# Linear-attention state summed over four token tiles per burst instead of two, with two more buffers per ring in a weight slot

## The chip, the cores and the metric

The kernel runs on one core of a Trainium2 chip. The metric is the device time of one execution in microseconds (us). The profile's span is about 1.8 us shorter than the time of the same run.

## The reference, cut to what matters

```python
# A: linear attention, B: dilated sliding-window attention, both on the same x (2048 x 1024, 32 heads of 32)
pq, pk = phi(q), phi(k)                       # phi(t) = where(t > 0, t + 1, exp(t)) + 1e-6
kv = einsum("bhsd,bhse->bhde", pk, v)         # the state: a 32 x 32 sum over all 2048 tokens, per head
z  = einsum("bhsd->bhd", pk)
a  = (pq @ kv) / (pq @ z + 1e-6) @ A_wo
b  = windowed_attention(x) @ B_wo
g  = sigmoid((x * gate_w).sum(-1, keepdims=True))
return g * a + (1 - g) * b
```

## The kernel before

The program is recorded as a list of operations with reads and writes. A list scheduler in Python then fixes the order of each engine before anything is built: an operation's place follows from its dependencies, a planned cost and a priority. The state stage walks over 16 tiles of 128 tokens. For each it computes the features of the keys (`pk`, two groups of eight matmuls) and the values with a column of ones (`az`, two groups). The sum over tokens needs both. A "burst" is the operation that does it: 32 small matmuls per tile, in four column tiles of the tensor engine, whose records overlap in the trace (64 matmuls of 182 ns each start within 0.48 us). In the code, a bank is one of the buffers that matmuls write to, evacuation is the copy of a result out of its bank, `r` counts the four groups of a tile, and `KVAT` is 1.

```python
    pk = Ring([SB([128, 1024], BF16, "pk%d" % i) for i in range(4)])
    az = Ring([SB([128, H, 33], BF16, "az%d" % i) for i in range(4)])
# ... cut ...
        def state(two):                        # the tiles of one burst
            bank = main.next()
            def fn(e):
                for s in range(8):
                    for i, (t, pkt, azt) in enumerate(two):
                        for c in range(4):
                            h = 16 * (s // 4) + 4 * c + s % 4
                            last = e.matmul(bank.ap()[32 * c:32 * c + 32, s * 33:s * 33 + 33], pkt[:, h * 32:(h + 1) * 32], azt[:, h, :],
                                            start=(i == 0), stop=(i == len(two) - 1), tile_position=(0, 32 * c))
                return last
            # ... cut: add() gathers the bank into kva on VectorE ...

        def run_state():
            fn, rd, bank, add = state([states.pop(0)[1] for _ in range(2)])
            P.op("pe", fn, 0.55, mode="k", reads=rd, writes=[bank.iv], name="kv")
            add()

        for t in range(NT):
            # ... cut: the four groups of the tile, their evacuation, attention blocks of B in between ...
                if r == KVAT and t % 2 and t > 1:
                    run_state()

        def last_state():
            run_state()
            totals()
        after(1, last_state)                   # the last burst, one group into the next stage
        load_w(3, 0, Bo, 0, 50)                # B's output weight, 2 MB, as soon as slot 3 is free
        load_w(3, 1, Bo, 512, 51)
```

The attention of B runs in between, in "attention bursts": scores of one block and values of the block before, 32 + 64 small matmuls in 64 x 64 tiles. The folding of the state into A's output weight comes later, in four bursts of 16.

## Time and profile before

| | kernel before |
|---|---|
| time, 3 runs ahead of the prediction | 484.12 us (484.1 to 484.35) |
| span in the profile | 482.1 us |
| tensor engine busy, share of the last chain | 98%, 95% |
| state bursts | 8 of 64 matmuls, 0.70 us each |
| DVE, ACT busy | 58%, 31% |

In the profile, PE is the matmul row of the tensor engine, PEld its weight loads, DVE and ACT are VectorE and ScalarE, SPq is the queue that issues transfers. L1343 is a full-array matmul, L1450 and L1485 are attention's scores and values, L1579 is the state (L1574 after the change). The lines that carry the reading are shown in the prediction.

### The profile page before, as it was taken

To read this page: it belongs to the slowest core of one execution; us is meant where nothing else is said; L and a number is where in the kernel's file an instruction comes from. 1 tells how busy PE (TensorE), PEld (TensorE's weight loads), DVE (VectorE), ACT (ScalarE), POOL (GpSimd) and SP (SyncE) were. 2 spreads that over 40 slices of the span, in tenths; PEclk is the share of its full clock that TensorE was granted. 3 is DMA by queue.
4 is the path that set the end of the run, shared out by engine and by line. 5 is a ranking of instruction groups with operands and counts; after the bars stand their busy time and mean duration, and the time that the engine had idled before them with its cause. 6 is when DMAs were issued, how large, how long until landed. Compare 5 with 4: busy or idle time off the path is not lost.

```text
span 482.1 us, 10165 instructions
## 1 busy us (share of the span) xinstructions
PE 472.3 (98%) x4349; PEld 224.3 (47%) x4403; DVE 280.3 (58%) x578; ACT 149.3 (31%) x238; POOL 5.8 (1%) x36
## 2 busy tenths in 40 slices
PE   8999999999999999999999999999999999999997
PEld 3444444444444544545444555444444444444443
DVE  2121435878687788565747565697489136653434
ACT  2111111235333345435434335345532130111000
POOL 4000000000000000000000000000000000000000
DMA  8999992232014359742213414720186019840212
GB/s 225 218 215 311 357 363 46 65 111 87 1 33 141 87 139 203 163 82 69 76 43 83 101 33 99 215 46 1 15 223 156 0 17 235 228 24 2 88 68 90
DMA packets 72951, 57.39 MB, mean 119 GB/s; under 512 B 37953, under 2 KB 60865, under 8 KB 72898
## 3 DMA queue, kind: packets, MB, share of 16 engines
q1 hardware_dynamic: 72210, 56.07, 45.0%
q8 instruction: 36, 0.59, 0.5%
q10 hardware_dynamic: 688, 0.59, 0.4%
q14 instruction: 17, 0.14, 0.1%
HBM read 34.49 MB, written 13.76 MB: 100 GB/s over the span
## 4 chain that ended last, share of the span: by engine, by line
PE 95%; DVE 2%; ACT 1%; issue 1%
PE ps_all L1343 77%; PE ps_all L1729 11%; PE ps_all L1485 2%; PE ps_all L1450 2%; ACT E L1464 1%; PE ps_all L1382 1%; DVE E L1467 1%; DVE pk L1356 1%; PE ps_all L1579 0%; PE ps_all L1674 0%; DVE qd L1440 0%; PE ps_all L1646 0%; DVE e L1354 0%; DVE rs L1501 0%; DVE ot L1502 0%
## 5 line engine op out<-in xcount | busy, mean ns | idle before, releaser
L1343 PE MATMUL ps_all<-w,xT 128*128 128x512 bf16 x930 | 206.9, 380 | 3.7 <-issue 2.5
L1343 PE MATMUL ps_all<-xT,w 128*128 128x512 bf16 x750 | 165.8, 379 | 1.8 <-issue 1.3
L1343 PEld LDWEIGHTS ps_all<-w,xT 128*128 128x128 bf16 x960 | 92.3, 98 | 110.1 <-issue 1.6
L1343 PEld LDWEIGHTS ps_all<-xT,w 128*128 128x128 bf16 x768 | 74.2, 98 | 89.4 <-issue 1.3
L1729 PE MATMUL ps_all<-w,qT 128*128 128x512 bf16 (+1 forms) x260 | 55.4, 372 | 0.2
L1729 PEld LDWEIGHTS ps_all<-w,qT 128*128 128x128 bf16 x264 | 25.9, 98 | 29.6
L1374 DVE CAST vst<-ps_all 128x512 bf16<-128x512 f32 x15 | 10.4, 694 | 43.1 <-PE ps_all L1343 43.1
L1464 ACT ACTIVATE E<-ps_all 128x1824 bf16<-128x1824 f32 (+1 forms) x18 | 30.4, 1687 | 14.1 <-PE ps_all L1485 14.1
L1354 DVE TENSOR_SCALAR e<-e 128x512 bf16<-128x512 bf16 x64 | 18.5, 289 | 27.4 <-ACT e L1352 13.7
L1733 DVE SCALAR_TENSOR_TENSOR o<-ps_all,gm,xT 128x512 bf16<-128x512 f32 (+1 forms) x25 | 18.0, 728 | 21.1 <-PE ps_all L1729 21.0
L1352 ACT ACTIVATE e<-ps_all 128x512 bf16<-128x512 f32 x32 | 19.1, 597 | 34.8 <-PE ps_all L1343 34.8
L1350 ACT ACTIVATE e<-ps_all 128x512 bf16<-128x512 f32 x32 | 19.1, 597 | 27.6 <-PE ps_all L1343 26.5
L1302 DVE TENSOR_TENSOR mx<-mx,kT 128x1024 bf16<-128x1024 bf16 x32 | 21.0, 684 | 9.8 <-ACT kT L1375 9.6
L1502 DVE TENSOR_TENSOR ot<-ps_all,rs 128x480 bf16<-128x480 f32 (+1 forms) x54 | 25.8, 505 | 0.0
L1375 ACT ACTIVATE az<-ps_all 128x512 bf16<-128x512 f32 x24 | 14.4, 599 | 36.2 <-PE ps_all L1343 36.2
L1501 DVE RECIPROCAL rs<-ps_all 128x15 f32<-128x15 f32 (+1 forms) x54 | 9.4, 203 | 27.8 <-PE ps_all L1485 25.9
L1302 DVE TENSOR_TENSOR mx<-mx,qT 128x1024 bf16<-128x1024 bf16 x32 | 21.0, 684 | 6.8 <-ACT qT L1378 6.7
L1375 ACT ACTIVATE vst<-ps_all 128x512 bf16<-128x512 f32 x17 | 10.2, 599 | 47.5 <-PE ps_all L1343 47.5
L1375 ACT ACTIVATE kT<-ps_all 128x512 bf16<-128x512 f32 x21 | 12.5, 596 | 36.0 <-PE ps_all L1343 36.0
L1378 ACT ACTIVATE qT<-ps_all 128x512 bf16<-128x512 f32 x20 | 11.9, 597 | 34.4 <-PE ps_all L1343 34.4
L1356 DVE SCALAR_TENSOR_TENSOR pk<-ps_all,e 128x512 bf16<-128x512 f32 x32 | 21.6, 678 | 0.2
L1378 ACT ACTIVATE xT<-ps_all,g 128x512 bf16<-128x512 f32 x10 | 6.9, 687 | 45.1 <-PE ps_all L1343 45.1
(73 smaller groups left out, 276.8 us busy)
## 6 DMA issues: line engine op xcount, KB each, us to landing
rb<-rc_hbm SPq DMA_DIRECT2D x32, 256.0 KB, 5.9
w<-in_A_wqkv_dram SPq DMA_DIRECT2D x6, 1024.0 KB, 8.8
v<-vB_hbm SPq DMA_DIRECT2D x36, 132.0 KB, 2.9
vB_hbm<-vst SPq DMA_DIRECT2D x32, 132.0 KB, 5.8
w<-in_B_wqkv_dram SPq DMA_DIRECT2D x4, 1024.0 KB, 8.3
xn<-in_A_x_dram SPq DMA_DIRECT2D x16, 256.0 KB, 2.6
out_dram<-o SPq DMA_DIRECT2D x15, 256.0 KB, 2.2
oB_hbm<-ot SPq DMA_DIRECT2D x36, 96.0 KB, 2.2
```

The costliest lines, as they stand in the source:

```text
L1302: P.op("dve", lambda e, m=m, op=op: e.tensor_tensor(m[:, 0:n], m[:, 0:n], src, op), 0.08 + n / 1920.0, reads=[m.all(), reg], writes=[m.all()],
L1343: last = e.matmul(bank.ap(), lhs(dc), rhs(dc), start=(dc == 0), stop=(dc == 7))
L1350: P.op("act", lambda e: e.activation(e_[:, :], bank.ap(), ACT.Exp), act(512), reads=[bank.iv], writes=[e_.all()])
L1352: P.op("act", lambda e: e.activation(e_[:, :], bank.ap(), ACT.Exp, accum_out=qe[:, col:col + 1]), act(512) + 0.1, reads=[bank.iv], writes= ...
L1354: P.op("dve", lambda e: e.tensor_scalar(e_[:, :], e_[:, :], 1.0, 1e-6, op0=ALU.min, op1=ALU.add), 0.25, reads=[e_.all()], writes=[e_.all()])
L1356: P.op("dve", lambda e: e.scalar_tensor_tensor(out=dst, in0=bank.ap(), scalar=0.0, in1=e_[:, :], op0=ALU.max, op1=ALU.add), dps(512), read ...
L1375: fa = lambda e: e.activation(dst, src(), ACT.Copy)
L1378: fa = lambda e: e.activation(dst, src(), ACT.Copy, scale=scale)
L1464: P.op("act", lambda e: e.activation(E[:, 0:32 * nq].rearrange("p (j q) -> p j q", j=4), ps[:, 4:8, 0:8 * nq], ACT.Exp), act(32 * nq), rea ...
L1502: P.op("dve", lambda e, r=r, src=src, dst=dst, m=m: e.tensor_tensor(dst, src()[:, :, 0:32], r[:, 0:m, None].to_broadcast([128, m, 32]), AL ...
L1729: last = e.matmul(bank.ap(0, f1 - f0), qT[:, dc, t * 128:(t + 1) * 128], ws[3][:, dc, f0:f1], start=(dc == 0), stop=(dc == 7))
L1733: P.op("dve", lambda e, bank=bank, o_=o_, t=t, n=n, i0=i0, i1=i1, tgt=tgt, c0=c0: e.scalar_tensor_tensor(out=o_[:, i0 * 128:i1 * 128].rear ...
```

## The change

Its intent: the tensor engine is the bound, and each burst makes it change its tiling mode twice; half as many bursts pay half as many changes (0.225 us for the two in the trace of before, which is what a burst costs beyond the time from its first start to its last). Four tiles per burst were taken to need six buffers instead of four, and the only free place is the slot of B's key weights, which is later filled with A's output weight. So that load moves behind the last burst that uses the two new buffers.

```diff
-    pk = Ring([SB([128, 1024], BF16, "pk%d" % i) for i in range(4)])
-    az = Ring([SB([128, H, 33], BF16, "az%d" % i) for i in range(4)])
+    pk = Ring([... 4 as before ...] + [SB([128, 1024], BF16, "pk%d" % i, at=ws[1].lo + 2048 * (i - 4)) for i in (4, 5)])
+    az = Ring([... 4 as before ...] + [SB([128, H, 33], BF16, "az%d" % i, at=ws[1].lo + 4096 + 2112 * (i - 4)) for i in (4, 5)])
@@ at the end of the projections
-        for c in range(4): for I in range(2):   # A's output weight into ws[1], 8 transfers of 256 KB
-                P.op("sp", ... A_wo ..., prio=40, chan="wo%d_%d" % (c, I), lat=0.9)
@@
         def run_state():
-            fn, rd, bank, add = state([states.pop(0)[1] for _ in range(2)])
-            P.op("pe", fn, 0.55, mode="k", reads=rd, writes=[bank.iv], name="kv")
+            fn, rd, bank, add = state([states.pop(0)[1] for _ in range(4)])
+            P.op("pe", fn, 1.03, mode="k", reads=rd, writes=[bank.iv], name="kv")
             add()
+        def load_wo():                          # the same 8 transfers
@@
-                if r == KVAT and t % 2 and t > 1:
+                if r == KVAT and t % 4 == 0 and t:
                     run_state()
+                    if t == 12:
+                        load_wo()
```

(The first two lines are shortened, and the transfers' access patterns are left out.)

More of the change, by code (lines that the diff above doesn't have):

```diff
@@ L1215, in build_kernel @@
     mx = [SB([128, 1024], BF16, "mx%d" % i, at=ph + 2048 * i) for i in range(2)]
-    pk = Ring([SB([128, 1024], BF16, "pk%d" % i) for i in range(4)])
-    az = Ring([SB([128, H, 33], BF16, "az%d" % i) for i in range(4)])
+    pk = Ring([SB([128, 1024], BF16, "pk%d" % i) for i in range(4)] + [SB([128, 1024], BF16, "pk%d" % i, at=ws[1].lo + 2048 * (i - 4)) for i in (4, 5)])
+    az = Ring([SB([128, H, 33], BF16, "az%d" % i) for i in range(4)] + [SB([128, H, 33], BF16, "az%d" % i, at=ws[1].lo + 4096 + 2112 * (i - 4)) for i in (4, 5)])
     warm = SB([128, 512], BF16, "warm", at=pk.t[2].lo)
@@ L1558, in plan @@
         top_end(1, ALU.min)
-        for c in range(4):
-            for I in range(2):
-                P.op("sp", lambda e, c=c, I=I: e.dma_start(ws[1][32 * c:32 * c + 32, 4 * I:4 * I + 4, :],
-                                                           A_wo[512 * I + 128 * c:512 * I + 128 * c + 128, :].rearrange("(r e) f -> e r f", e=32)), 0.6,
-                     writes=[ws[1].part((4 * I, 4 * I + 4), (0, 1024))], prio=40, chan="wo%d_%d" % (c, I), lat=0.9)
         load_w(2, 0, Aw, 0, 42)
@@ L1591, in run_state @@
         def run_state():
-            fn, rd, bank, add = state([states.pop(0)[1] for _ in range(2)])
-            P.op("pe", fn, 0.55, mode="k", reads=rd, writes=[bank.iv], name="kv")
+            fn, rd, bank, add = state([states.pop(0)[1] for _ in range(4)])
+            P.op("pe", fn, 1.03, mode="k", reads=rd, writes=[bank.iv], name="kv")
             add()
+        def load_wo():
+            for c in range(4):
+                for I in range(2):
+                    P.op("sp", lambda e, c=c, I=I: e.dma_start(ws[1][32 * c:32 * c + 32, 4 * I:4 * I + 4, :],
+                                                               A_wo[512 * I + 128 * c:512 * I + 128 * c + 128, :].rearrange("(r e) f -> e r f", e=32)), 0.6,
+                         writes=[ws[1].part((4 * I, 4 * I + 4), (0, 1024))], prio=40, chan="wo%d_%d" % (c, I), lat=0.9)
         for t in range(NT):
```

## The prediction

> **What bounds the kernel now.** I read the page's first and fourth parts, then the chain in order of time, then the groups by form, then the timeline of the tensor engine around single state bursts, and last the DMA queue of the weight that moves.
>
> ```profile
> PE 472.3 (98%) x4349; PEld 224.3 (47%) x4403; DVE 280.3 (58%) x578; ACT 149.3 (31%) x238; POOL 5.8 (1%) x36
> ...
> PE 95%; DVE 2%; ACT 1%; issue 1%
> ```
>
> The tensor engine is 98% busy and carries 95% of the chain that ended last. DVE and ACT have room. A busy matmul row can hide slack, so the rate has to be checked. The chain in order of time:
>
> ```profile
> 14.82 10.74 PE ps_all L1343 x49
> 25.61 10.74 PE ps_all L1343 x49
> ```
>
> Two pieces of 50 matmuls each start 10.79 us apart: 0.2158 us per 512-column matmul. Wherever I checked from 129 us on, the start-to-start spacing of the full-array matmuls is this number, with extra time only around bursts of small tiled matmuls (scores and values of attention, the linear-attention state, the fold, the denominators). So the span is nearly a sum: full matmuls at 0.2158 us plus a fixed cost for each burst. A change pays by what it takes out of that sum; work taken from DVE, ACT or DMA pays only if a stall is there, and there is almost none.
>
> The state work, in the groups by form:
>
> ```profile
> L1579 PE MATMUL ps_all<-az,pk 128*32 128x33 bf16 x512 | 5.3, 182 | 0.0
> L1579 PEld LDWEIGHTS ps_all<-az,pk 128*32 128x32 bf16 x512 | 4.5, 93 | 3.4 <-DVE e L1354 2.5 <-issue 0.4 <-DVE ot L1502 0.4
> L1588 DVE TENSOR_TENSOR kva<-ps_all,kva 128x264 f32<-128x264 f32 x7 | 3.0, 423 | 0.6 <-PE ps_all L1579 0.6
> ```
>
> 512 matmuls in 8 bursts of 64; seven adds (and one copy) gather them. The 3.4 us of weight-load idle is 8 times 0.42 and is named after DVE, but I don't read it as a wait for data: the array still streams the last full matmuls in that time. What a burst costs is read from the matmul timeline:
>
> ```profile
> 300.57 3.40 PE L1343 MATMUL ps_all<-w,xT 128*128 128x512 bf16 x15 [0.16 <-issue]
> 303.90 0.67 PE L1579 MATMUL ps_all<-az,pk 128*32 128x33 bf16 x64
> 304.73 0.59 PE L1343 MATMUL ps_all<-w,xT 128*128 128x512 bf16 x2 [0.16 <-issue]
> ```
>
> and the weight loads of the same stretch:
>
> ```profile
> 300.34 3.14 PEld L1343 LDWEIGHTS ps_all<-w,xT 128*128 128x128 bf16 x16
> 303.90 0.57 PEld L1579 LDWEIGHTS ps_all<-az,pk 128*32 128x32 bf16 x64 [0.42 <-DVE e L1354]
> ```
>
> Sixteen weight loads but fifteen matmuls: the first matmul after each burst has no record. Counting the visible gaps on both sides would therefore charge a whole matmul (0.216 us) to the burst. Between the two first records (300.57 and 304.73, both second matmuls of their run) lie 4.16 us with 16 full matmuls, 16 x 0.2158 = 3.45. The burst costs 0.70 us. The same subtraction gives 0.701 to 0.705 for all eight, so none of them waits for anything that another leaves out.
>
> [...] of the 0.70 us, 0.48 lies between the first and the 64th start of the burst, and 0.225 is left for going in and coming back. [...] in every burst the first 32 matmuls [...] start within 0.218 us, 6.8 ns each, and from there on the step is a steady 8.46 ns[...]. [...] The trace shows 36 packets and 0.59 MB on an instruction queue, so 16 KB each; a burst of 128 pairs is just such a block.
>
> **The change part by part.**
>
> 1. Bursts. Before: 8 bursts of 64 matmuls. After: 4 of 128; the number of matmuls is the same, 512. All lies on the tensor engine, which is the bound. One new burst is 0.218[...] + 95 steps x 8.46 ns = 1.022 us, plus 0.225 for the two mode changes: 1.247 us. Two old ones are 1.406. Saved: 0.16 us for each pair, 4 x 0.16 = 0.64 us. It is this small because merging saves a pair of mode changes (0.225) but gives 0.06 of it back[...].
>
> 2. Adds on DVE. Four of the eight go: 4 x 0.42 = 1.7 us. DVE is at 60% in this stage and no matmul waits for it; worth 0.
>
> 3. Two more buffers in each ring, in the slot of the B key weights. The four-tile burst needs them, as it holds four tiles while the next is written. The first burst comes about two groups (3.5 us) after the last of its data is computed; evacuating that takes 0.60 us on ACT or 0.69 on DVE, so no wait. Fourth-tile data before were older still, which saved nothing.
>
> 4. The A output weight (2 MB, 8 transfers) moves from the end of the projection stage to after the third burst.
>
> ```profile
> 174.00:194.00 20.00, 19.68 (x274) 9.82 (x275) 15.98 (x41) 10.04 (x12) 0.00 (x0) 1.00 1.00 195
> 277.00:289.00 12.00, 11.68 (x207) 6.03 (x208) 7.82 (x19) 4.68 (x6) 0.00 (x0) 1.00 0.10 28
> 289.00:301.00 12.00, 11.68 (x236) 6.27 (x237) 6.03 (x18) 5.76 (x8) 0.00 (x0) 1.00 0.42 103
> 301.00:313.00 12.00, 11.58 (x236) 5.95 (x238) 7.81 (x20) 4.30 (x8) 0.00 (x0) 1.00 0.72 217
> ```
>
> The last two columns are DMA share and GB/s. Today it is fetched between 174 and 194 us, where the DMA engines are full at 195 GB/s, and the tensor engine is not held up even there: the attention bursts of that stretch cost 1.15 to 1.26 us against the usual 1.145. In the new place, from some 280 us, the engines are at a tenth. My estimate from 195 GB/s is about 11 us of transfer, landing near 292; the first fold reads it at 319.8. Slack 27 us. Worth 0 at the new place, and at most the 0.1 us of one slow attention burst at the old.
>
> 5. The last burst is 0.54 us longer (64 x 8.46 ns) and the fold depends on it. Today its add starts at 312.98 and the transposed state is ready by 314.8, 5 us before the fold; half a microsecond doesn't reach it.
>
> Sum: 484.12 - 0.64 = 483.48, which I round to 483.5.
>
> **The rivals.**
>
> A. The visible gaps were right and a merge saves more. With 0.309 and 0.344 us read at the burst's two ends, one would get 0.92 per burst and 1.5 us in all: 482.6. Against it speak the sixteen loads to fifteen matmuls. A variant: 7.6 ns average per matmul for the second half too gives 0.225 x 4 = 0.9 us, 483.2.
>
> B. The merged burst waits, for the fourth tile's values or for a bank. A wait of one evacuation, 0.6 to 0.7 us, in each of three bursts would cost up to 2 us: 485.5. For it: the fourth tile is fresh where the tiles of before were old. Against it: two groups of slack, and ACT and DVE have no attention exponentials to do in the fourth tile of each four, since none is issued there.
>
> C. The moved weight delays the value loads of the last attention blocks or comes late for the fold; a stall of 1 to 5 us, 485 to 488. Against it: values are loaded about 16 us ahead, twice the burst of weight traffic, and the tensor engine stood 20 us of full DMA traffic before.
>
> D. Instruction fetch. Three attention bursts of the old kernel (195.7, 226.6, 299.7) hold one gap of 50 to 93 ns and a few smaller ones. A burst of 256 instructions is 1.3 times theirs (192) and may meet one or two more: +0.1 to 0.3 us.
>
> E. The order of instructions is found by a list scheduler at build time, so removing four operations can shuffle others: a group swapped around a burst, another neighbour for a burst. One mode-change pair more or less is 0.2 us; I allow 0.5 either way.
>
> **Range and chances.** The sum gives 483.5. A lowers the lower end to 482.6, D and E with a little of B raise the upper end to 484.3; eight in ten should lie there. Two per cent is 9.7 us. All eight bursts together cost 8 x 0.70 = 5.6 us, so faster by 2% is out of reach of the change itself: 1%. Slower by 2% needs C in a form that nothing shows: 1%. Within 2%: 98%.
>
> **What the new profile should show.** Four state bursts of 128 matmuls, one each some 31 us apart, each with a cost by the same subtraction near 1.25 us (right), above 1.4 (no gain), or near 1.1 (the average rate holds). Full-array spacing stays 0.2158 us. Steps after the 32nd matmul stay at 8.46 ns up to the 128th. The gathering adds fall to three and one copy, with no matmul gaining by it. The A output weight is issued near 280 us and no fold waits for it. I am wrong if the matmul row shows a stall ahead of a state burst named after ACT or DVE of more than 0.2 us, if the attention bursts after 280 us cost more than 1.3 us, or if the time moves by more than 1 us while the bursts' costs come out as said; then the order of something else has changed.

Cut in it, at the marks, are the author's reasons for the cost of a mode change and for the two rates of starts, which no trace or run shows, and a size of the instruction blocks that was not taken from the traces. The trace of before shows 0.218 us to the 33rd start, 8.46 ns a start beyond and 0.225 us left for going in and coming back, so a burst of 128 comes to 1.247 us and the sum to 484.12 - 0.64 = 483.48. The 0.06 us given back are the second 64 matmuls taken at 8.46 ns throughout, where the first 32 of a burst of their own start at 6.8. That a burst of 128 pairs is about a block of instructions is an estimate from the traces: between two of the first 34 fetches lie 127.1 loads on average before the change and 126.8 after, so 254 matmuls and loads; with some two semaphore instructions (64 and 67 records beside the 4403 loads) that is about 256, the figure used below.

## The result, and the profile after

| | before | after |
|---|---|---|
| median of 6 runs each | 484.18 us (483.92 to 484.57) | 484.37 us (483.97 to 484.78) |
| span in the profile | 482.1 us | 483.0 us |

A ratio here is the one of the two kernels' fast runs in the same rounds; it is not quite the ratio of the medians. It is 1.0003, with a 95% interval of 0.999 to 1.0016: the same. 483.5 was predicted with a range up to 484.3; the median lies 0.07 us above the range, and the 0.64 us that should have been saved are not in the time.

The page after the change, engines and chain:

```profile
PE 478.1 (99%) x4403; PEld 223.7 (46%) x4403; DVE 279.6 (58%) x575; ACT 148.7 (31%) x237; POOL 6.2 (1%) x38
...
PE 96%; SPq 2%; DMA 1%; issue 0%; DVE 0%
```

The matmul row grew by 5.8 us because all 4403 matmuls have a record this time, where 54 were missing before (a second trace of the changed kernel, with 50 missing, has 471.6 us). The bound is the same engine. The new entries of SPq and DMA are at the start of the kernel. The groups of the state by form:

```profile
L1574 PE MATMUL ps_all<-az,pk 128*32 128x33 bf16 x512 | 4.9, 184 | 0.2 <-issue 0.2
L1574 PEld LDWEIGHTS ps_all<-az,pk 128*32 128x32 bf16 x512 | 4.4, 93 | 2.0 <-issue 2.0
L1583 DVE TENSOR_TENSOR kva<-ps_all,kva 128x264 f32<-128x264 f32 x3 | 1.3, 433 | 1.0 <-PE ps_all L1574 1.0
```

Three adds instead of seven. The load row's idle time should be 4 x 0.42 = 1.7 us and is 2.0, and the matmul row, which had none, has 0.2 us "issue": time in which the engine waited for nothing that the profile shows. The second burst in the timeline of matmuls:

```profile
245.71 1.03 PE L1343 MATMUL ps_all<-w,xT 128*128 128x512 bf16 x4
246.67 1.20 PE L1574 MATMUL ps_all<-az,pk 128*32 128x33 bf16 x128
247.80 1.47 PE L1343 MATMUL ps_all<-w,xT 128*128 128x512 bf16 x6
```

128 matmuls in one record, and full matmuls again 1.13 us after its start. With 0.09 us of entry (the last full matmul ahead started 0.309 us before the burst, and takes 0.216) that is 1.22. By the subtraction that the prediction uses, which ends at the second full matmul after the burst, it is 1.235, close to the predicted 1.247; all costs below are of this kind. The last burst, in the same view:

```profile
310.18 1.89 PE L1343 MATMUL ps_all<-xT,w 128*128 128x512 bf16 x8
312.00 1.06 PE L1574 MATMUL ps_all<-az,pk 128*32 128x33 bf16 x111
313.25 0.30 PE L1574 MATMUL ps_all<-az,pk 128*32 128x33 bf16 x17 [0.20 <-issue]
313.48 7.08 PE L1343 MATMUL ps_all<-xT,w 128*128 128x512 bf16 x32
```

It is cut in two. After 111 matmuls the engine stands for 0.38 us, start to start, then does the other 17. Its whole cost is 1.48 + 0.09 = 1.57 us (1.587 by the subtraction). No semaphore shows there: in the program all waits of a burst stand ahead of its first matmul, and in the trace, too, the first of the 128 is the only one that carries a wait.

Where the 0.9 us of the longer span came from, read from the starts of single records, in three parts. The start, up to the first attention burst, took 130.17 us instead of 129.09. The middle, from there to the last matmul, took 349.59 instead of 350.02. The end, from there on, took 3.29 instead of 3.02. The order of the built programs is the same for the tensor engine and the transfer queue until long after the start-up loads (in the traces, up to weight load 1699 of the tensor engine and to 174 us on the transfer queue), so the change has no hand in the first part; in the twelve traces that part runs from 129.09 to 130.17, and the trace of the kernel before happens to have the shortest. It has the shortest end, too: 3.02 to 3.33 in the twelve, without a pattern that follows the change. The change is to be judged by the middle: 0.43 us saved of the 0.64.

### The profile page after: what moved, and what is told of

It reads as the page before. It is cut to its first block, busy times and chain, and to the rows that moved or that the text cites. A ratio compares the mean times of both kernels' runs of the same rounds, so it can differ in the third digit from the quotient of the medians.

```text
span 483.0 us, 10222 instructions
## 1 busy us (share of the span) xinstructions
PE 478.1 (99%) x4403; PEld 223.7 (46%) x4403; DVE 279.6 (58%) x575; ACT 148.7 (31%) x237; POOL 6.2 (1%) x38
## 4 chain that ended last, share of the span: by engine, by line
PE 96%; SPq 2%; DMA 1%; issue 0%; DVE 0%
PE ps_all L1343 79%; PE ps_all L1733 11%; PE ps_all L1450 2%; PE ps_all L1485 2%; SPq L1317 1%; DMA w<-in_B_wqkv_dram 1%; PE ps_all L1574 1%; SPq L1322 1%; PE ps_all L1678 0%; PE ps_all L1650 0%; DVE o L1737 0%
## 5 line engine op out<-in xcount | busy, mean ns | idle before, releaser
L1343 PE MATMUL ps_all<-w,xT 128*128 128x512 bf16 x960 | 212.2, 380 | 0.5 <-DMA xT<-in_A_x_dram 0.4
L1343 PE MATMUL ps_all<-xT,w 128*128 128x512 bf16 x768 | 168.3, 380 | 0.0
```

The lines of the kernel that those rows point to most:

```text
L1343: last = e.matmul(bank.ap(), lhs(dc), rhs(dc), start=(dc == 0), stop=(dc == 7))
```

## The experiments

The theory: the sum of burst costs holds, and what is missing from the gain is the gap inside the last burst; the start is chance. The rivals: the changed kernel itself starts slower; the moved weight holds something up; a long burst in that place has the gap for a reason of its own. The "middle" below is always the time from the first attention burst to the last matmul. The state column is the sum over all state bursts by the subtraction. There is one trace of each kernel where the table doesn't say more. How far the middle can be trusted shows in the three traces whose tensor-engine order is that of the kernel before: 349.84 to 350.02. The times are given with the number of runs.

| kernel | state bursts, us | gap in a state burst | middle, us | median, us | before, same rounds |
|---|---|---|---|---|---|
| before | 5.62 | none | 350.02 | 484.18 (6) | |
| changed, three traces | 5.29, 6.33, 5.29 | 0.38, 1.42, 0.39 us | 349.59, 350.78, 349.58 | 484.37 (6), 484.81 (6), 484.24 (5) | 484.18, 484.50, 484.11 |
| last burst split | 5.90 | 0.81 us | 350.17 | 485.10 (5) | 484.50 |
| pairs, buffers and load moved | 5.61 | none | 349.96 | 484.51 (5) | 484.50 |
| fours, four buffers | 5.69 | 0.14, 0.66 us | 350.52 | 484.69 (6) | 484.50 |
| changed, B's weight late, two traces | 4.94, 4.94 | none | 349.20, 349.24 | 483.73 (5), 483.77 (5) | 484.08, 484.11 |
| before, B's weight late | 5.61 | none | 349.84 | 484.31 (5) | 484.08 |
| changed, instructions shifted | 4.99 | none | 349.27 | 483.84 (1) | 484.08 |
| single tiles | 7.40 | 0.32 us | 351.48 | 486.12 (1) | 484.08 |

### The changed kernel again

No edit.

> The changed kernel once more, unaltered. Theory 1 (the sum of burst costs holds; what is missing from the predicted gain is one gap of 0.35 us inside the last state burst, and a start-up stall of some 0.8 us that comes by chance in some executions of either kernel): three state bursts cost 1.235 us each, the last 1.58 with the gap at the same matmul, the times fall into two groups some 0.7 us apart for both kernels, and group against group the changed kernel is 0.2 to 0.4 us faster. Theory 2 (the start-up stall belongs to the changed kernel): only the changed kernel has the upper group, and the kernel before stays within 0.3 us. Theory 3 (the moved weight load holds something up): attention bursts after 275 us cost more than the usual 1.145 us.

Measured: ratio 1.0001 (0.9988 to 1.0015). The three full bursts cost 1.234 to 1.236 us, the last 2.62: the gap stands at the same matmul and is 1.42 us long this time. The matmul timeline of that burst:

```profile
311.70 1.06 PE L1574 MATMUL ps_all<-az,pk 128*32 128x33 bf16 x111
313.99 0.29 PE L1574 MATMUL ps_all<-az,pk 128*32 128x33 bf16 x17 [1.23 <-issue]
```

The kernel before spread nearly as widely in these rounds (483.64 to 485.03 in 11 runs, against 483.73 to 485.35 in 6), so the wide spread does not belong to the changed kernel, and that rival falls; the two clean groups of times that I had expected did not appear either. Attention bursts after 275 us cost up to 1.26 us here but no more than 1.15 in the first trace; the moved weight is no steady cost.

What the place of the gap means shows when the tensor engine's weight loads are counted from the start of the program: the gap follows load 3530 in each of the three traces. Each matmul has one load, and the page's instruction queue shows 36 packets of 16 KB, by the mean distance of two fetches (126.8 loads) about 256 instructions or 128 pairs each. That suggests a fetch that comes late; the next runs test it.

### The last burst split

```diff
+                if r == KVAT and t == 15:
+                    run_state(2)
 ...
         def last_state():
-            run_state()
+            run_state(2)
```

> The last four-tile burst is split into two of two tiles, placed as before; the other three stay merged. Theory 1: state bursts cost 3 x 1.235 + 2 x 0.703 = 5.11 us in all (changed kernel 5.29, kernel before 5.62), no gap inside a burst, so 0.5 us less than the kernel before and 0.2 us less than the changed kernel, outside the start-up. If the gap of the last burst came from where it stands and not from its length, one of the two small bursts still has it and costs about 1.05 us.

The first expectation failed, and the second branch held. The matmul timeline of the last burst, now of two tiles:

```profile
310.57 0.59 PE L1574 MATMUL ps_all<-az,pk 128*32 128x33 bf16 x55
311.79 0.24 PE L1574 MATMUL ps_all<-az,pk 128*32 128x33 bf16 x9 [0.63 <-issue]
```

It has a gap of 0.81 us after its 55th matmul, and load 3530 of the program is just this 55th. So the gap follows neither the burst's length nor the place in the burst: it stays at one place of the instruction stream. The small burst costs 1.50 instead of 0.70 us, and the kernel is slower than the one before (ratio 1.0022, 1.0008 to 1.0036).

### Pairs, with the buffers and the load moved

```diff
-            fn, rd, bank, add = state([states.pop(0)[1] for _ in range(4)])
+            fn, rd, bank, add = state([states.pop(0)[1] for _ in range(2)])
-                if r == KVAT and t % 4 == 0 and t:
+                if r == KVAT and t % 2 and t > 1:
-                    if t == 12:
+                    if t == 13:
```

> Two-tile bursts as in the kernel before, but with the six buffers and the output weight loaded late. Its tensor-engine order is that of the kernel before, instruction for instruction. Theory 1: eight bursts at 0.70 us, the time is that of the kernel before within 0.2 us. Theory 3: slower than the kernel before by 0.3 us or more, with attention bursts above 1.2 us or a wait for the output weight after 275 us.

Eight bursts at 0.70 us, middle 349.96, ratio 0.9999 (0.9986 to 1.0013). Buffers and late load of A's weight cost nothing and give nothing that these runs can show. That rival falls.

### Fours with four buffers

A's output weight is loaded at the old place, the rings have four buffers, and a burst stands ahead of the next tile's first write:

```diff
-                if r == KVAT and t % 4 == 0 and t:
+                if r == 3 and t % 4 == 3 and t < NT - 1:
```

> Four-tile bursts with the four buffers of the kernel before and the output weight loaded where it was. If the extra buffers are needed, each burst has to wait for the values of its fourth tile and the next tile's features wait for the burst: a stall of 0.5 to 2 us at three places, time 1 to 4 us above the kernel before. If the slack of PSUM covers it, bursts cost 1.24 us with no wait and the time is that of the changed kernel within 0.3 us.

The second branch held in the main: no wait of the tensor engine on ACT or DVE at a burst, two middle bursts at 1.234 us, and ratio 1.0006 (0.9992 to 1.0019). So the two extra buffers and the moved load were not needed for bursts of four. Its first burst has a gap of 0.14 us that I did not follow up, and the last has 0.66 us, ending 1.27 us after a block's fetch, between load 3531 and its matmul (one instruction later than in the others; a stream with one instruction less ahead of it would make it the same place, which I did not show). One attention burst (188 us) has a gap of 0.34 us too.

### The changed kernel with B's output weight late

The theory could be made sharper. From the transfer records of the instruction queue, the last fetch ahead of the gap, taken to be that of the block in which the stream goes on after load 3530, began at 310.77, 311.71 and 309.44 us in the first three traces with a gap, and the gap ended 1.51, 1.34 and 1.31 us after the end of that fetch. That is in the 303 to 312 us in which the 2 MB of B's output weight fill the engines (the data queue takes 97.7% of the 16 engines' time in the first trace). Hence the test: take the traffic away.

```diff
         def last_state():
-            run_state()
+            last_kv = run_state()
+            load_w(3, 0, Bo, 0, 50, after=[last_kv])
+            load_w(3, 1, Bo, 512, 51, after=[last_kv])
             totals()
 ...
-        load_w(3, 0, Bo, 0, 50)
-        load_w(3, 1, Bo, 512, 51)
```

> The changed kernel with one thing held back: the B output weight (2 MB) is loaded after the last state burst instead of from 303 us on, when the engines' queues are full while a block of tensor instructions is being fetched. Theory 1, now sharper (the tensor engine runs out of instructions at one fixed place, load number 3530 of its stream, because the fetch of that block waits behind the weight): [...]the last burst costs 1.24 us, all four 4.95 us, no gap inside it, and from the first attention burst to the last matmul it is 0.35 us or more shorter than the changed kernel (349.6 us) and 0.6 to 0.8 us shorter than the kernel before (350.0 us). Rival (the gap belongs to a long burst in this place, whatever the DMA does): the gap stays at the same matmul.

The clause cut in it had the fetch come earlier than 310.8 us, at a place that followed from a view of what starts a fetch, which was not shown.

The last burst in the matmul timeline:

```profile
311.42 1.20 PE L1574 MATMUL ps_all<-az,pk 128*32 128x33 bf16 x128
312.77 1.46 PE L1343 MATMUL ps_all<-xT,w 128*128 128x512 bf16 x6 [0.16 <-issue]
```

The gap is gone: the burst costs 1.235 us by the subtraction (the first full matmul after it has no record), and all four cost 4.94. The DMA queues from 305 to 309.5 us, first in the changed kernel, where no instruction fetch begins in that stretch (queue and kind: packets, MB, share of the engines):

```profile
q1 hardware_dynamic: 1331, 1.35, 98.8%
```

and from 309.5 to 312.5 us, still in the changed kernel, where it does:

```profile
q1 hardware_dynamic: 1022, 0.93, 90.6%
q8 instruction: 1, 0.02, 2.0%
```

With B's weight late, 305 to 309.5 us:

```profile
q1 hardware_dynamic: 1265, 0.45, 59.5%
q8 instruction: 1, 0.02, 1.3%
```

The data queue has gone from 98.8% to 59.5%, and the block comes in that stretch, at 306.97 us instead of 310.77: 3.8 us earlier, and its transfer ends 4.4 us ahead of its use. The place in the stream tells the same. With the weight held back the fetch begins as load 3400 does (0.17 us after it), some 130 loads, about one block, ahead of load 3531; in the changed kernel it begins 3.40 us after load 3400. A trace shows when a fetch begins, not when it was asked for; that it was asked for near load 3400 in both is an inference from the same stream of instructions. How the DMA engines divide their time between the two queues no trace shows; the runs show the later fetch beside the fuller data queue.

The middle is 349.20 us, 0.39 below the changed kernel's first and 0.82 below that of the kernel before. Of the 0.82 the state bursts make 0.68; the rest is as large as the spread of the middle. The ratio to the kernel before is 0.9991 (0.9977 to 1.0004).

### The same hold-back in the kernel before

> The same hold-back in the kernel before, as a control. Theory 1: it had no gap in its state bursts, so nothing changes there: eight bursts at 0.70 us, first attention burst to last matmul 350.0 us within 0.2. If the late weight helps in some other way, it is shorter here too.

No gap, eight bursts at 0.70 us, middle 349.84, ratio 0.9999 (0.9985 to 1.0012): no gain from the late weight where no gap was. Yet the fetch moves here as well, from 309.97 to 306.89 us. So the block was late in the kernel before too. There load 3530 is the 47th of a burst of 64, and load 3531 was needed 1.60 us after the fetch's end: just outside the 1.26 to 1.51 us at which gaps end. The kernel before escapes by 0.1 to 0.3 us.

### The instruction stream shifted

75 more warm-up matmuls at the very start, narrow ones, so that the start takes about as long:

```diff
         for i in range(WARM):
-            P.op("pe", lambda e: e.matmul(banks[7].ap(), warm[:, 0:128], warm[:, :], start=True, stop=True), 0.43, ...)
+            def warm_fn(e, i=i):
+                if i < 2:
+                    return e.matmul(banks[7].ap(), warm[:, 0:128], warm[:, :], start=True, stop=True)
+                for _ in range(10 if i < 5 else 9):
+                    last = e.matmul(banks[7].ap(0, 48)[0:32, :], warm[:, 0:32], warm[:, 0:48], start=True, stop=True)
+                return last
+            P.op("pe", warm_fn, 0.43, ...)
```

> The changed kernel with 75 more (narrow) warm-up matmuls at the start, so 150 more tensor instructions ahead of everything; the weight is loaded where the changed kernel loads it. The ends of the 256-instruction blocks move 150 instructions earlier against the work: the end that stood at the 112th matmul of the last burst now stands at its 37th. Theory 1: [...]no gap in the last burst (1.24 us), or a gap that stands at the 37th matmul; in no case at the 112th. Rival (place and length): the gap stays at the 112th matmul. The whole time is not to be compared, as the start is changed.

The clause cut in it, with a landing by about 309 us, rested on the same view of what starts a fetch, which was not shown. The 256 instructions of a block are the estimate from the traces that stands beside the prediction, and the end at the 112th matmul is where the gap stood (load 3531).

The last burst in the matmul timeline (L1580 is the state in this kernel):

```profile
311.39 1.25 PE L1580 MATMUL ps_all<-az,pk 128*32 128x33 bf16 x128
```

No gap at the 112th matmul and none at the 37th; the last burst costs 1.29 us. B's weight is loaded where the changed kernel loads it, and the data queue is as full (96.7% from 305 to 309.5 us). The block that the burst crosses into was fetched at 301.15 us, before that weight, and was there 9.2 us ahead of its use. The steps after the 108th matmul are a little ragged, up to 19 ns, which makes the 0.05 us. The middle is 349.27 us, that of the late weight. Same burst, same place, same traffic, other alignment: no gap. The rival of a long burst in that place falls.

### Bursts of a single tile

```diff
-            fn, rd, bank, add = state([states.pop(0)[1] for _ in range(2)])
+            fn, rd, bank, add = state([states.pop(0)[1]])
-                if r == KVAT and t % 2 and t > 1:
+                if r == KVAT and t:
```

> Sixteen bursts of one tile, 32 matmuls each, in the kernel before. It tests the law of the burst's cost, 0.225 us for the two mode changes, 6.8 ns a start for the first 32 and 8.46 ns for each beyond: 0.225 + 31 x 6.8 ns = 0.44 us each, 7.0 us in all against 5.6 for pairs. If the cost were a fixed 0.225 and the average 7.6 ns: 0.46 us each. If each mode change cost the 0.31 us that the visible gaps suggest, 0.85 us each.

Fifteen of the sixteen bursts cost 0.414 to 0.418 us, nearest to the first law (0.44), below the second and far below the third. With 32, 64 and 128 matmuls at 0.415, 0.703 and 1.235 us, the second 32 add 9.0 ns each and the next 64 add 8.3 ns each. One burst, at 199 us, costs 1.17: it has a gap of 0.32 us at another place (after load 1618), which ends 1.48 us after the end of a block's fetch, again with the DMA engines full (a share of 0.99 or more from 190 to 198 us). The rest of its excess is not settled.

### The two versions side by side

> The changed kernel a third time, beside the one with the late B output weight on the same chip. Late instruction block (theory 1): three bursts at 1.235 us, the last one longer by 0.3 to 1.5 us with its gap again at load number 3530, ending 1.3 to 1.5 us after the fetch of that block; median within 0.4 us of the kernel before.

> The changed kernel with the late B output weight once more. Theory 1: four bursts at 1.235 us, no gap, and from the first attention burst to the last matmul 349.2 us again (0.8 below the first trace of the kernel before); median 0.3 to 0.8 us below that of the kernel before and 0.4 to 1.2 us below that of the changed kernel in the same rounds. If the first result was luck, the medians lie within 0.2 us.

The changed kernel: gap of 0.39 us after load 3530, ending 1.26 us after the end of the block's fetch, last burst 1.587 us, median 484.24 us, ratio 1.0003 (0.9988 to 1.0017). With the late weight: no gap, 4.94 us, middle 349.24, median 483.77 us, ratio 0.9990 (0.9976 to 1.0004). Medians lie 0.47 us apart. Each interval alone still includes 1, so by times alone the version is not proved faster; but both say the same, and all ten of its runs are at or below 483.98 us, which 5 of the 18 runs of the kernel before in those rounds are. That it is faster rests on the traces: no gap in two of two, where the changed kernel has one in three of three. It is the version that I would keep.

## Why the prediction was right or wrong, point by point

- **What bounds the kernel.** Right. The sum of full matmuls and bursts accounts for the middle part: less the state bursts it is 344.1 to 344.5 us in eleven of the twelve traces, and 344.8 in the one whose attention burst has a gap of 0.34.
- **The missing first record.** Right, and it mattered. The full trace after, where no record is missing, gives the same 1.235 us as the traces with missing records, and the single-tile bursts rule out the cost that the visible gaps suggest.
- **Step 1, the bursts.** Right in its arithmetic: 1.247 us predicted per burst, 1.233 to 1.237 measured in every burst without a gap, but for 1.29 in the ragged one of the shifted kernel; four of them 4.94 us against eight at 5.62, so 0.68 us saved where 0.64 was predicted. One reading is slightly off: 0.218 us is the start of the 33rd matmul, the 32nd starts after 0.20, which is why the single-tile bursts cost 0.415 and not 0.44. Wrong for the last burst of the changed kernel, which was taken to be like the others.
- **Step 2, DVE.** Right: no matmul gained by it.
- **Step 3, the buffers.** Right that no burst waits for its fourth tile. The sentence that the buffers are needed is wrong: with four of them the bursts wait for nothing either.
- **Step 4, the moved weight.** Right: issued from 280 us, nothing waits for it. Its last transfer was issued at 292.2 us and such a transfer took 3.1 to 4.5 us to land, so it was there near 296 and not 292, with 24 us of slack. But the reason that I gave, that the tensor engine had stood full DMA traffic before, was the wrong comfort. It can stand it where a block holds full matmuls: 127 of them (the mean distance of two fetches, in loads) last 27 us at 0.2158 us each, an estimate beside which a fetch 3 to 5 us late is still in time. It didn't where a burst runs through a block. The transfer that hurts was one I had not looked at: B's output weight at 303 us, which the change does not touch.
- **Step 5, the longer last burst.** Right that it doesn't reach the fold: even with the gap the transposed state was ready at 315.6 us and the fold began at 320.5.
- **Rival D, instruction fetch, is the step that failed.** It named the right mechanism and sized it by the wrong lines: gaps of 50 to 93 ns in attention bursts, so "+0.1 to 0.3 us". The term measured 0.38, 1.42 and 0.39 us in three traces of the changed kernel, so the last burst cost 1.59, 2.62 and 1.59 us and not 1.247. Taken off the 0.68 us, that leaves a gain of 0.3, a loss of 0.7 and a gain of 0.3: about nothing, which is what the times say. The right estimate would have put the fetch of each block beside the time of its use. In the trace of before, the block for load 3531 had ended 1.60 us ahead of its use, while the burst of 128 starts its first 111 matmuls, with their loads 222 of a block's about 256 instructions, in 0.9 us.
- **Rivals A, B, C.** None came about. The marks set for them (a stall named after ACT or DVE, attention bursts above 1.3 us, a wait for A's weight) were not seen in the changed kernel.
- **Rival E, another order.** It did not come about to any size: the middle less the state bursts is 344.40 us before and 344.26 to 344.45 in the five traces of the changed kernel with and without the late weight.
- **The range.** It was too narrow for a metric in which single executions of one kernel spread over 1.4 us (483.6 to 485.03 for the kernel before); three close runs had suggested 0.25 us. The median's 0.07 us above the range may be this spread; the missing gain is the gap.

What stays open: what exactly starts the fetch of a block, and why the gaps end only 1.3 to 1.5 us after the end of the transfer. The runs show these numbers, not their cause. For the start they show a place: near load 3400 (3398 to 3400) in the three traces with B's weight held back, 2.5 to 4.6 us after that load in the seven in which the weight was in flight at that moment. The small gaps inside attention bursts near 196 and 204 us, some 0.1 us in several kernels, were not looked into.

## What to carry to other kernels

Where the bound engine issues many short instructions in a burst, its instructions are data that have to arrive too: find the ends of the instruction blocks in the burst (16 KB each here, and about 256 instructions by the mean distance of two fetches, 127 loads), and keep bulk loads out of the few microseconds in which the next block is fetched. Merging bursts saves the mode changes (0.225 us a pair here) but makes the burst eat a block faster, so that a fetch that was just in time comes late (here it ended 1.60 us ahead of its use in the kernel before, and the changed kernel stood for 0.38 us). And a gap labelled "issue" that stays at the same instruction number when the work around it is changed points to a fetch, not a wait on data; here holding back the transfers and shifting the stream showed it.
